# ConvNeXt-V2 block: three of eleven blocks kept whole in DRAM, the others recomputed whole

## The chip, the cores and the metric

One core of one Trainium2 chip. The time is the device time of one launch in microseconds (us). The kernel before has a median of 1508.93 us over 7 runs (1504.76 to 1513.4).

## The reference

`x` is a picture of 512 x 512 pixels with 96 channels in bf16. The block is a depthwise 3 x 3 convolution, a layer norm over the channels, a matmul to 384 channels, a tanh gelu, a global response norm (GRN) and a matmul back to 96 channels, with a residual:

```python
out = sum over i, j of xp[:, i:i+H, j:j+W, :] * dw[i, j]      # depthwise 3x3
h = _gelu(einsum('bhwc,ce->bhwe', _layernorm(out), w1))
gx = jnp.sqrt((h * h).sum(axis=(1, 2), keepdims=True) + 1e-6) # over the whole picture
nx = gx / (gx.mean(axis=-1, keepdims=True) + 1e-6)
h = grn_gamma * (h * nx) + grn_beta + h
return x + jnp.einsum('bhwe,ec->bhwc', h, w2)
```

`gx` needs the gelu outputs of every pixel before the second matmul can start. So the picture is gone over twice.

## The kernel before

The picture is cut into 128 blocks of 4 rows (2,048 pixels). A block is four quarters ("quads") of 512 pixels; the 384 middle channels are three chunks of 128 (`NCH`).

**First pass.** It runs in slots, about one block per slot, each engine following an order written out by hand (`InOrder`, so line 32, where the helper records the call, stands for most instructions). For slot s: SP loads x rows of block s+4 (`load_x`); VectorE transposes the rows of block s+2 into channel-major form (`turn_x`, into `xT`); TensorE does the convolution of block s from three neighbouring `xT` (`conv_taps`, into `Y`); ScalarE evacuates it (`y_bf`). GpSimd squares it (`ysq`), TensorE sums (`SG`), and every four blocks the reciprocal standard deviation is worked out on GpSimd (`stage_rstd`, `stage_newton`), turned by VectorE, written to DRAM and read back spread over the partitions (`rbc`, `stage_rows`, `stage_bcast`). GpSimd multiplies (`yn`, `stage_norm`), SP writes `yn` to DRAM (`stage_write`) and reads it back in channel order (`ynT`, `stage_read`).

A few slots later the block has its MLP (`mlp_units`): nine units, each some matmuls with `w1p` into a PSUM tile `U` of one or two banks, and one gelu on ScalarE. Quads 0 and 1 come channel-major into `gsh`, and quad 2 channel-major and quad 3 pixel-major into `gm`. The sum of squares for `gx` is taken in two ways. Channel-major quads get `bn_stats` on VectorE (`squares`, `squares_rest`, three per quad: nine a slot). The pixel-major quad gets Gram products on TensorE (`gram_mms`: 12 matmuls of 128 x 128 whose diagonal is the sum), half of them in each of two places of the next slot. `cm_quads` says how many quads of a block are channel-major: 3, and 2 for the last two blocks.

Quad 0 of each block is stored to DRAM by SP in the next slot (`store`, 384 KB of `g_dram`). The last two blocks (`RES`) keep two quads in SBUF (`resg`).

**Between the passes** VectorE turns the sums into the GRN scale and scales `w2` into `W2s`, while TensorE and ScalarE already recompute quads of the two resident blocks (`ahead`).

**Second pass.** The blocks are gone through in `ORDER`, the two resident ones first. At iteration n:
- `stage_load` (line 234) for block n+5: `gl`, the stored quad, on SP, or on GpSimd's queue for every third block (line 242); `ynT`, the other three quads of the normalised input, on SP (line 245), 768 bytes per row and partition; `xr`, the rows of x, on GpSimd's queue (line 247). `gl` has six buffers, `xr` five, `ynT` six.
- `stage_xb` (line 275) for block n+2: GpSimd adds the bias to `xr` (`xb`, line 279, three buffers).
- `stage_mm2` (line 283) for block n: four subs, each 12 matmuls with `W2s` into a tile `O`, VectorE adds `xb` to give `o_sb`, and then `pace` (line 331) issues further recompute units: three matmuls of 512 columns into `U` and one gelu of 1,536 elements per partition into `gr`. A block has three such units, each one chunk of channels over three quads.
- `stage_out` (line 309) writes the finished block on SP.

These second-pass DMAs and `xb` aren't under the hand-written order; the scheduler places them on their queues.

Of the kernel before, what the change touches and what calls it, by code (L numbers as in the profile page):

```python
# [9 lines left out]
ACTF = mybir.ActivationFunctionType  # L10
# [8 lines left out]
RES = 2  # L19

# [33 lines left out]
def kernel(  # L54
# [29 lines left out]
    g_dram = dram.tile([NBLK, 128, NCH * QW], bf16, name="g_dram")  # L84
# [5 lines left out]

    def cm_quads(q):
        return 2 if is_res(q) else 3

    def kept_quads(q):
        return 2 if is_res(q) else 1
# [16 lines left out]
    def yn_rows(q):  # L112
        k = kept_quads(q) * 128
        return yn_dram[q:q + 2].rearrange("q c (r w) -> (q c) r w", r=GR)[0:128, :, k:]
# [30 lines left out]
    res_g = {q: prepool.tile([128, 2, NCH, QW], bf16, name=f"resg{q}") for q in range(NBLK - RES, NBLK)}  # L145
# [7 lines left out]
    ORDER = list(range(NBLK - RES, NBLK)) + list(range(NBLK - RES))  # L153

    class late:
        pass
# [3 lines left out]
    with ExitStack() as p1:  # L160
        pe, dve, act, pool, sp = (InOrder(tc, e) for e in (nc.tensor, nc.vector, nc.scalar, nc.gpsimd, nc.sync))
        gshpool = p1.enter_context(tc.tile_pool(name="gsh", bufs=3))
        gmpool = p1.enter_context(tc.tile_pool(name="gm", bufs=3))
# [70 lines left out]
        def stage_load(n, sq, pq):  # L234
            q = ORDER[n]
            v = (ORDER[0] + n) % NYT
            r0 = q * GR
            if is_res(q):
                kept, ynt = res_g[q], ynts[q]
            else:  # L240
                kept = late.gl.tile([128, 1, NCH, QW], bf16, name="gl")
                (pq if q % 3 == 0 else sq).dma_start(  # L242
                    out=kept[:].rearrange("p t j w -> p (t j w)"), in_=g_dram[q])
                ynt = yn_ring[v]
                sq.dma_start(out=ynt[:, :, kept_quads(q) * 128:], in_=yn_rows(q))
            xr = late.xr.tile([128, PXP, C], bf16, name="xr")
            pq.dma_start(out=xr[:], in_=x[0, r0:r0 + GR].rearrange("r w c -> (r w) c").rearrange(  # L247
                "(p g) c -> p g c", g=PXP))
            grp[q] = dict(kept=kept, ynt=ynt, xr=xr)

        def recompute_units(q):
            nk = kept_quads(q)
            ynt = grp[q]["ynt"]

            def fresh(j):
                if j == 0:
                    grp[q]["made"] = late.gr.tile([128, NCH, (NQ - 1) * QW], bf16, name="gr")
                def half(U, t0, t1):
                    for t in range(t0, t1):
                        pe.matmul(quad_out(U[:, t - t0, :]), lhsT=w1p[:, j * 128:(j + 1) * 128],  # L260
                                  rhs=quad(ynt[:], t), start=True, stop=True)
                    act.activation(out=grp[q]["made"][:, j, (t0 - nk) * QW:(t1 - nk) * QW],
                                   in_=U[:, :t1 - t0, :].rearrange("p k w -> p (k w)"), func=ACTF.Gelu_apprx_tanh)

                if not is_res(q):
                    half(late.psU2.tile([128, NQ - 1, QW], f32, name="U2"), nk, NQ)
                elif j % 2:
                    half(banks(1), nk, nk + 1)
                    half(banks(1), nk + 1, NQ)
                else:  # L270
                    half(banks(2), nk, NQ)

            return [lambda j=j: fresh(j) for j in range(NCH)]
# [9 lines left out]
        def stage_mm2(n, q):  # L283
            kept, made, xb = grp[q]["kept"], grp[q]["made"], grp[q]["xb"]
            nk = kept_quads(q)
            GQ = QW // 128
            o_sb = late.o.tile([128, PXP, C], bf16, name="o_sb")
            for sub in range(NSUB):
                O = late.psO.tile([128, GPS, C], f32, name="O")
                for gl_ in range(GPS):  # L290
                    gg = sub * GPS + gl_
                    for j in range(NCH):
                        t, c = gg // GQ, gg % GQ * 128
                        if t < nk:
                            lhsT = kept[:, t, j, c:c + 128]
                        else:
                            c += (t - nk) * QW
                            lhsT = made[:, j, c:c + 128]
                        pe.matmul(O[:, gl_, :], lhsT=lhsT, rhs=W2s[:, j, :],
                                   start=(j == 0), stop=(j == NCH - 1))  # L300
                dve.tensor_tensor(out=o_sb[:, sub * GPS:(sub + 1) * GPS, :], in0=O[:],
                                   in1=xb[:, sub * GPS:(sub + 1) * GPS, :], op=ALU.add)
                if n == NBLK - 1:
                    out_part(q, o_sb, sub)
                pace(n, sub)
            grp.pop(q)
            return o_sb
# [8 lines left out]
        UPB = NCH  # L316
        LEAD = RES * UPB + 2
        todo = [n for n in range(NBLK) for _ in range(UPB)]
        total = len(todo)
        made = [0]  # L320
        waiting = []

        def advance(target, upto):
            while made[0] < total and made[0] < target and todo[made[0]] < upto:
                n = todo[made[0]]
                if not waiting:
                    waiting.extend(recompute_units(ORDER[n]))
                waiting.pop(0)()
                made[0] += 1

        def pace(n, sub):
            due = sum(1 for v in todo if v <= n + 1) if sub == NSUB - 1 else 0
# [287 lines left out]
        gms = {}  # L620
# [4 lines left out]

        def mlp_units(b):
            gsh = res_g[b] if is_res(b) else gshpool.tile([128, 2, NCH, QW], bf16, name="gsh")
            gms[b] = gmpool.tile([128, TAIL], bf16, name="gm")
# [5 lines left out]
            def unit(bank, n):  # L634
                U = banks(n)
                if bank < 2 * NCH:
# [3 lines left out]
                    act.activation(out=gsh[:, t0:t0 + n, j, :], in_=U[:], func=ACTF.Gelu_apprx_tanh)  # L640
# [4 lines left out]
                while c < end:  # L645
                    if c < px0(b):
                        j, sz = c // QW, QW
                        cm_mm(Uf[:, c - c0:c - c0 + sz], j, 2)
# [8 lines left out]
                act.activation(out=gms[b][:, c0:end], in_=Uf, func=ACTF.Gelu_apprx_tanh)  # L657

            def entry(j, m, src):
# [3 lines left out]
                dve.bn_stats(out=bsts[k][:, j, e, :], in_=src)  # L663

            def squares(j):
                for m in range(2):
                    entry(j, m, gsh[:, m, j, :])

            def squares_rest():
                if px0(b):  # L670
                    for j in range(NCH):
                        entry(j, 2, gms[b][:, j * QW:(j + 1) * QW])

            def store():
                sp.dma_start(out=g_dram[b], in_=gsh[:, 0].rearrange("p j w -> p (j w)"))

            return unit, squares, squares_rest, store

        def gram_mms(b, part=None):
            n = (TAIL - px0(b)) // E  # L680
            for k in range(n) if part is None else range(n // 2) if part == 0 else range(n // 2, n):
                for j in range(NCH):
                    c = px0(b) + k * E + j * 128
                    v = gms[b][:, c:c + 128]
                    pe.matmul(gram[:, j, :], lhsT=v, rhs=v, start=False, stop=True, skip_group_check=True)
# [17 lines left out]
        for k, (b0, n) in enumerate(BATCHES):  # L703
# [16 lines left out]
            for b in range(b0, b0 + n):  # L720
# [7 lines left out]
                put(m, "combine", b)  # L728
                put(m + (b < NBLK - 1), "gram", b)
# [5 lines left out]
        store = None  # L735
        for s in range(last_slot + 1):
# [11 lines left out]
            if store:  # L748
                store()
                store = None  # L750
# [18 lines left out]
            if not mlp:  # L769
                if s + 2 < NBLK:  # L770
                    turn_x(s + 2)
# [19 lines left out]
                for b in get("gram"):  # L791
                    gram_mms(b)
            else:
                b = mlp[0]
                unit, squares, squares_rest, put_out = mlp_units(b)
                conv = lambda n, fence=True: taps[n](fence) if taps else None

                def gram_of_last(part):
                    for b2 in get("gram"):
                        if b2 != b:  # L800
                            gram_mms(b2, part)
# [7 lines left out]
                if s + 2 < NBLK:  # L809
                    turn_x(s + 2)  # L810
# [3 lines left out]
                gram_of_last(0)  # L814
# [8 lines left out]
                gram_of_last(1)  # L823
# [7 lines left out]
                squares_rest()  # L831
                for b2 in get("gram"):
                    if b2 == b:
                        gram_mms(b2)
                if not is_res(b):
                    store = put_out
# [8 lines left out]
            if s == last_slot - 3:  # L845
# [4 lines left out]
                late.gr = p2.enter_context(tc.tile_pool(name="gr", side="right", bufs=4))  # L850
                late.gl = p2.enter_context(tc.tile_pool(name="gld", side="right", bufs=6))
# [6 lines left out]
        if store:  # L858
            store()
# [28 lines left out]
        ahead = [f for n in range(RES) for f in recompute_units(ORDER[n])]  # L888
        for f in ahead[:-1]:
            f()  # L890
# [16 lines left out]
        ahead[-1]()  # L907
        made[0] = RES * UPB
# [53 lines left out]
```

## Time and profile before

| | |
|---|---|
| median of 7 runs | 1508.93 us |
| the profiled execution | 1507.57 us, its span 1505.8 us |
| PE busy | 1414.8 us (94%) |
| ACT busy | 1451.5 us (96%) |
| DVE busy | 1194.0 us (79%) |
| POOL busy | 1309.8 us (87%) |
| DMA moved | 427.10 MB, 284 GB/s on average |

PE is TensorE, ACT ScalarE, DVE VectorE, POOL GpSimd, SP the sync engine that issues DMAs. The busy tenths in 40 slices of the span show the two passes: DVE falls at the 25th slice, DMA rises to 9 there:

```profile
DVE  7759999999999999999999989755555555455555
ACT  7898999999999999999999999999999999899997
POOL 3469899999999999999999987299999999899998
...
DMA  6668787888887887888888677899999999999996
```

The first pass ends at about 965 us, the second runs from about 972 us. Busy counts an engine that runs an instruction, so several engines can be full at once. What sets the time is read from the waits, stage by stage.

### The profile page before, as it was taken

How to read it: one execution, taken by the hardware profiler on the slowest of the kernel's cores; microseconds unless marked ns; L12 is line 12 of the kernel's file. 1: busy time of each engine (PE TensorE's matmuls, PEld its weight loads, DVE VectorE, ACT ScalarE, POOL GpSimd, SP SyncE). 2: the span in 40 equal slices, each digit the busy share in tenths (PEclk: the TensorE clock that was granted, in tenths of full speed). 3: DMA queues.
4: the chain of work that ended last, by engine and by line, in shares of the span. 5: the costliest groups of instructions: out<-in, count | busy, mean ns of one | idle time of the engine just before them, and what ended most of it. 6: DMA issues, size and time to landing. Idle time of an engine off the chain costs nothing. (4 is left out here: it accounts for less than half of the span.)

```text
span 1505.8 us, 54858 instructions
## 1 busy us (share of the span) xinstructions
PE 1414.8 (94%) x23110; PEld 815.7 (54%) x23110; DVE 1194.0 (79%) x2149; ACT 1451.5 (96%) x1699; POOL 1309.8 (87%) x934
## 2 busy tenths in 40 slices
PE   8888999999999999999999987799999999999998
PEld 3434444444444444444444443477777776676766
DVE  7759999999999999999999989755555555455555
ACT  7898999999999999999999999999999999899997
POOL 3469899999999999999999987299999999899998
PEclk9999999999999999999999999999999999999999
DMA  6668787888887887888888677899999999999996
GB/s 177 177 189 258 238 254 240 255 255 242 251 250 245 251 254 237 256 262 247 251 265 248 206 206 249 260 342 391 377 385 390 375 378 378 364 367 383 378 378 237
DMA packets 235181, 427.10 MB, mean 284 GB/s; under 512 B 34006, under 2 KB 148278, under 8 KB 234934
## 3 DMA queue, kind: packets, MB, share of 16 engines
q1 hardware_dynamic: 219972, 356.59, 73.3%
q0 software_dynamic: 13600, 66.86, 11.7%
q8 instruction: 181, 2.97, 0.8%
q14 instruction: 66, 0.54, 0.1%
q10 hardware_dynamic: 1362, 0.15, 0.1%
HBM read 272.78 MB, written 150.72 MB: 281 GB/s over the span
## 5 line engine op out<-in xcount | busy, mean ns | idle before, releaser
L32 PE MATMUL U<-ynT,w1p 128*128 128x512 bf16 x2292 | 650.6, 381 | 38.7 <-ACT gsh L32 9.1
L32 ACT ACTIVATE gr<-U 128x1536 bf16<-128x1536 f32 (+1 forms) x386 | 519.1, 1449 | 12.5 <-PE U L32 10.8
L32 DVE BATCH_NORM_STATS2 bst<-gsh 128x6 f32<-128x512 bf16 x756 | 465.6, 673 | 17.6 <-ACT gsh L32 17.3
L32 DVE TENSOR_TENSOR o_sb<-O,xb 128x384 bf16<-128x384 f32 x512 | 278.0, 556 | 252.7 <-PE O L32 156.9
L32 POOL TENSOR_TENSOR yn<-y_bf,rbc 128x1536 bf16<-128x1536 bf16 x126 | 391.3, 3108 | 74.5 <-ACT rbc L32 21.8
L32 ACT ACTIVATE gm<-U 128x512 bf16<-128x512 f32 (+1 forms) x640 | 419.8, 801 | 5.9 <-PE U L32 5.7
L279 POOL TENSOR_TENSOR xb<-xr,B2c 128x1536 f32<-128x1536 bf16 x126 | 394.7, 3133 | 32.3 <-DVE B2c L32 26.5
L32 ACT ACTIVATE gsh<-U 128x1024 bf16<-128x1024 f32 x504 | 375.1, 871 | 7.5 <-PE U L32 5.6
L32 PE MATMUL Y<-xT,Wq 64*32 64x511 bf16 (+1 forms) x8694 | 321.7, 387 | 20.0 <-ACT y_bf L32 8.5
L32 POOL TENSOR_TENSOR ysq<-y_bf 128x1536 bf16<-128x1536 bf16 x114 | 313.6, 2752 | 11.4 <-ACT y_bf L32 11.4
L32 PEld LDWEIGHTS <-w1p 128*128 128x128 bf16 x2292 | 182.9, 98 | 242.7 <-issue 151.0
L32 PEld LDWEIGHTS <-gr 128*128 128x128 bf16 x4584 | 237.1, 98 | 106.1 <-issue 20.3
L32 PE MATMUL O<-W2s,gr 128*128 128x96 bf16 x4584 | 257.6, 206 | 11.4 <-DVE o_sb L32 10.8
L32 DVE BATCH_NORM_STATS2 bst<-gm 128x6 f32<-128x512 bf16 x378 | 232.9, 672 | 0.2 <-ACT gm L32 0.2
L32 PEld LDWEIGHTS <-Wq 64*32 64x32 bf16 x9216 | 112.9, 90 | 196.6 <-issue 148.5
L32 ACT ACTIVATE y_bf<-Y 128x1536 bf16<-128x1536 f32 x121 | 188.1, 1554 | 7.9 <-PE Y L32 4.0
L32 DVE STREAM_TRANSPOSE xT<-xin 128x576 f32<-128x576 f32 (+1 forms) x256 | 181.3, 749 | 0.0
L32 PEld LDWEIGHTS <-gm 128*128 128x128 bf16 x1560 | 99.7, 98 | 85.5 <-issue 53.5
L32 PE MATMUL SG<-gm 128*128 128x128 bf16 x1560 | 130.7, 221 | 1.8 <-DVE SG L32 1.2
L32 PE MATMUL U<-w1p,ynT 128*128 128x384 bf16 (+2 forms) x780 | 127.2, 272 | 1.4 <-ACT resg L32 0.2
L247 POOL DMA_DIRECT2D xr<-in_x_dram x123 | 68.1, 554 | 38.5 <-POOL xb L279 35.3
L32 PE MATMUL O<-W2s,gl 128*128 128x96 bf16 x1512 | 85.0, 206 | 0.0
(105 smaller groups left out, 673.4 us busy)
## 6 DMA issues: line engine op xcount, KB each, us to landing
ynT<-yn_dram SPq DMA_DIRECT2D x254, 384.0 KB
xin<-in_x_dram SPq DMA_DIRECT2D x126, 432.0 KB
yn_dram<-yn SPq DMA_DIRECT2D x512, 96.0 KB
xr<-in_x_dram POOLq DMA_DIRECT2D x128, 384.0 KB, 6.5
out_dram<-o_sb SPq DMA_DIRECT2D x127, 384.0 KB
g_dram<-gsh SPq DMA_DIRECT2D x126, 384.0 KB
gl<-g_dram SPq DMA_DIRECT2D x84, 384.0 KB
gl<-g_dram POOLq DMA_DIRECT2D x42, 384.0 KB, 7.2
```

The lines of the kernel that those rows point to most:

```text
L32: r = f(*a, **k)
L247: pq.dma_start(out=xr[:], in_=x[0, r0:r0 + GR].rearrange("r w c -> (r w) c").rearrange("(p g) c -> p g c", g=PXP))
L279: pq.tensor_tensor(out=xb[:], in0=grp[q]["xr"][:], in1=bias[:, None, :].to_broadcast([128, PXP, C]), op=ALU.add)
```

## The change

Which quads are stored changes from "quad 0 of each block" to "all four quads of three blocks of eleven". `WHOLE = (0, 4, 8)` names them by block number modulo 11 (35 of 126). The other blocks store nothing, and all four of their quads are recomputed in the second pass, the last two blocks included (`resg` is gone).

- Channel-major quads: a whole block has four (all its quads are then in the layout that the second pass wants), the block after it two, others three. The last three `bn_stats` of a whole block are put off to the next slot (`square_owed`). Gram products go through a list (`gram_next`), two entries of six matmuls a slot.
- `gsh` and `gm` become one tile `g` with four buffers. A whole block is stored as two halves of 768 KB, one in each of the next two slots (`store_next`).
- `turn_x` runs three slots ahead instead of two.
- Second pass: `gl` is a whole block (1,536 KB, two buffers, always on GpSimd's queue); `ynT` is loaded whole (4,096 contiguous bytes per partition) for the other blocks. A recompute unit is one quad with its three chunks: three matmuls and one gelu of 1,536 as before. `gr` has three buffers of a block; `pace` spreads the units evenly over all subs and keeps at least two quads ahead of the use.

```diff
+WHOLE = (0, 4, 8)
+GRB = 3
...
     def cm_quads(q):
-        return 2 if is_res(q) else 3
+        return NQ if is_whole(q) else 2 if is_res(q) or (q - 1) % 11 in WHOLE else 3
...
         def stage_load(n, sq, pq):
...
+            if is_whole(q):
+                grp[q]["g"] = late.gl.tile([128, NQ, NCH, QW], bf16, name="gl")
+                pq.dma_start(out=grp[q]["g"][:].rearrange("p t j w -> p (t j w)"), in_=g_dram[whole.index(q)])
             else:
-                kept = late.gl.tile([128, 1, NCH, QW], bf16, name="gl")
-                (pq if q % 3 == 0 else sq).dma_start(
-                    out=kept[:].rearrange("p t j w -> p (t j w)"), in_=g_dram[q])
-                ynt = yn_ring[v]
-                sq.dma_start(out=ynt[:, :, kept_quads(q) * 128:], in_=yn_rows(q))
+                ynt = yn_ring[(ORDER[0] + nth_made[q]) % NYT]
+                if not is_res(q):
+                    sq.dma_start(out=ynt[:], in_=yn_rows(q))
...
+        def recompute(q, t):
...
+            for j0, n in ((0, NCH),) if late.psU2 else ((0, 2), (2, 1)):
+                U = late.psU2.tile([128, NCH, QW], f32, name="U2") if late.psU2 else banks(n)
+                for j in range(j0, j0 + n):
+                    pe.matmul(quad_out(U[:, j - j0, :]), lhsT=w1p[:, j * 128:(j + 1) * 128],
+                              rhs=quad(ynt[:], t), start=True, stop=True)
+                act.activation(out=g[:, t, j0:j0 + n, :], in_=U[:, :n, :], func=ACTF.Gelu_apprx_tanh)
...
+        LEAD = 5
+        todo = [(n, t) for n in range(NBLK) if not is_whole(ORDER[n]) for t in range(NQ)]
...
+                if n >= upto or nth_made[ORDER[n]] >= used[0] + GRB:
+                    break
...
-            due = sum(1 for v in todo if v <= n + 1) if sub == NSUB - 1 else 0
+            soon = (n, sub + 2) if sub < NSUB - 1 else (n + 1, 1)
+            due = sum(1 for v in todo if v < soon or v[0] < n)
...
+        def store_next():
+            if stores:
+                b, h = stores.pop(0)
+                n = NCH * QW * 2
+                sp.dma_start(out=g_dram[whole.index(b)][:, h * n:h * n + n],
+                             in_=gs[b][:, 2 * h:2 * h + 2].rearrange("p t j w -> p (t j w)"))
...
-            if store:
-                store()
-                store = None
+            store_next()
...
-                if s + 2 < NBLK:
-                    turn_x(s + 2)
+                if s + 3 < NBLK:
+                    turn_x(s + 3)
...
-                squares_rest()
...
+                squares_rest(2)
+                square_owed()
+                if is_whole(b):
+                    owed.append(lambda f=squares_rest: f(3))
+                grams.extend((b, k) for k in range(0, (TAIL - px0(b)) // E, 2))
+                if is_whole(b):
+                    stores.extend(((b, 0), (b, 1)))
...
-                late.gr = p2.enter_context(tc.tile_pool(name="gr", side="right", bufs=4))
-                late.gl = p2.enter_context(tc.tile_pool(name="gld", side="right", bufs=6))
+                late.gr = p2.enter_context(tc.tile_pool(name="gr", side="right", bufs=GRB))
+                late.gl = p2.enter_context(tc.tile_pool(name="gld", side="right", bufs=2))
```

## The prediction

> **What bounds the kernel now.** First the busy time by stretch (engine: busy us and instructions of each stretch), one stretch of the first pass and one of the second:
>
> ```profile
> 500.00:600.00 100.00, 96.43 (x1749) 47.03 (x1741) 99.44 (x173) 99.77 (x142) 93.97 (x76) 1.00 0.80 247
> ...
> 1050.00:1100.00 50.00, 50.00 (x714) 36.88 (x711) 27.36 (x50) 50.00 (x39) 46.20 (x29) 1.00 1.03 375
> ```
>
> The columns are PE, PEld, DVE, ACT, POOL, clock, DMA share, GB/s. In the first pass ACT (99.77 of 100) and DVE (99.44) have no idle time; in the second DVE is half idle, and PE, ACT, POOL and DMA all look full. So each pass is read by its waits. First pass, waits of ACT from 300 to 900 us; then second pass, waits of DVE and of POOL from 1000 to 1450 us:
>
> ```profile
> ACT gm L32 <- PE U L32: 2.2, 2, 1.3
> ACT gsh L32 <- ACT gm L32: 1.1, 4, 0.5
> ...
> DVE o_sb L32 <- PE O L32: 130.7, 251, 1.7
> DVE o_sb L32 <- POOL xb L279: 84.1, 78, 3.5
> ...
> POOL xr L247 <- POOL xb L279: 31.5, 106, 0.3
> POOL xr L247 <- issue: 2.9, 1, 2.9
> ```
>
> ACT waits about 3 us in 600: the first pass is ACT's, 7.06 us a slot (600 us, 85 blocks). In the second pass DVE waits for POOL's xb, while POOL waits for nobody but itself: every xr issue stands 0.3 us behind the xb before it. POOL's timeline there:
>
> ```profile
> 1097.32 3.13 POOL L279 TENSOR_TENSOR xb<-xr,B2c 128x1536 f32<-128x1536 bf16 x1
> 1100.75 0.55 POOL L247 DMA_DIRECT2D xr<-in_x_dram  x1 [0.30 <-POOL xb L279]
> 1101.32 3.14 POOL L279 TENSOR_TENSOR xb<-xr,B2c 128x1536 f32<-128x1536 bf16 x1
> 1104.76 0.55 POOL L247 DMA_DIRECT2D xr<-in_x_dram  x1 [0.30 <-POOL xb L279]
> 1105.34 3.14 POOL L279 TENSOR_TENSOR xb<-xr,B2c 128x1536 f32<-128x1536 bf16 x1
> 1108.77 0.55 POOL L247 DMA_DIRECT2D xr<-in_x_dram  x1 [0.30 <-POOL xb L279]
> 1109.32 0.54 POOL L242 DMA_DIRECT2D gl<-g_dram  x1
> 1109.87 3.13 POOL L279 TENSOR_TENSOR xb<-xr,B2c 128x1536 f32<-128x1536 bf16 x1
> ```
>
> There is no hole: three blocks take 12.55 us (1097.32 to 1109.87), 4.18 a block, made of 4.005 for xb, wait and xr, and 0.54 for one gl in three blocks. PE alone would go at 4.03 (its block starts there are 1099.81, 1103.79, 1107.82, 1111.85), and ACT, at 27.00 us for 20 gelus of 1,536, at 3 x 1.345 = 4.03. So POOL sets the second pass, with PE and ACT 4% behind. DMA moves 379 GB/s from 1000 to 1450 us, close behind too.
>
> **What the Trainium skill says.** "DMA: Bandwidth & Descriptors", section on queues, rings and completion order: each DMA engine takes turns between the queues that have work, a packet at a time. The trace's records of single packets agree: at 1109 to 1114 us, packets of POOL's queue (6,144 bytes) and SP's (3,072 and 768) run side by side, POOL's at about 25 a us, 157 GB/s. Same page, on why small descriptors are slow: a fixed overhead per packet. The records agree: from 1000 to 1450 us a 768-byte packet took 36.4 ns (21.1 GB/s on its engine), a 3,072-byte one 129.8 ns (23.7), a 6,144-byte one 250.5 ns (24.5). Same page, anatomy of a SWDGE DMA: a POOL DMA costs some 2 us and its bytes over 436 GB/s, and descriptor generation is small. The page of this kernel has 6.5 us from issue to landing of an xr, where that gives 2.9: the engines are shared, so I use the trace.
>
> **The change, part by part**
>
> *First pass, ACT.* The same nine gelus and one evacuation per slot, same sizes: nothing. *DVE.* Per eleven blocks 3 x 4 + 3 x 2 + 5 x 3 = 33 quarters get bn_stats, as before; the last three of a whole block go to the next slot, whose own block has only two quarters, so each slot keeps nine. Over all blocks 383 quarters instead of 382: three more at 0.58 us (spacing in DVE's timeline), 1.7 us. *PE.* A px-major quarter costs six pieces of 1,536 columns in all, a channel-major one three of 512; the slot after a whole block gets one more px-major quarter, the whole one's slot one less. Gram products stay 12 a slot through the list. PE's slack (its waits sum to 8 us in 600) covers such 0.2 us shifts; if not, ACT waits that much in three slots of eleven.
>
> *Transposes one slot earlier.* xin(s+4) is issued at slot s and turned at s+1 instead of s+2. In the trace an xin issue at 605.63 is turned at about 624.3; now at 617.3, 11.7 us later instead of 18.7. Landing is not shown; eight packets of 3,456 bytes per engine at 181 ns are 1.5 us, plus what is queued ahead. Between 0 and some us in a slot; I take 0.
>
> *Stores.* 126 x 384 KB become 70 halves of 768 KB, in the two slots after a whole block, each at the place where the old store stood on SP. Such a slot moves about 384 KB more than now (some 280 GB/s instead of 247), the others 384 KB less. Behind a store stand the next xin, the ynT read and, every fourth slot, rbc, for which POOL's yn already waits now and then (11.2 us from 200 to 940 us). POOL is nearly full too: 4 x 5.84 + 4.5 = 27.9 us of work per 28.2 us of four slots. It can gain where slots without a store let such a wait go, at most those 11 us, and lose in store slots; I take 1 us lost in all, and keep 0.2 us for each of 70 slots, 14 us, for the range.
>
> *Second pass, ACT and PE.* 372 quads of 3 matmuls and one gelu instead of 382; in the loop 32 per 11 blocks instead of 33, at most three in any block, since the pace is even over blocks. ACT: 32/11 x 1.345 = 3.91 us a block. PE: 4 x 0.51 for the O products and 32/11 x 0.65 for U, 3.93. A quad is always issued two quads ahead of its use, and psU2 has two buffers, so no new wait for gelu.
>
> *POOL.* This is where the time is. The instruction order of the changed kernel, which can be read without running it, has 33 gl (all on POOL, 1,536 KB each) between the third xb and the last but four, where before had 40; and after each gl but one two xb follow each other and then two xr. The second xr's 0.30 us wait is gone in 32 such pairs, and xb after xb starts 3.09 us after the first (five take 15.45 at the end of the trace) instead of 3.13. Check on before: 121 x 4.005 + 40 x 0.54 = 506.2, and the waits of 3.5 for o_sb and 2.9 for issue make 512.6; the trace has 972.14 to 1484.25, 512.1. After: 506.2 - 7 x 0.54 - 32 x 0.34 = 491.5, that is 14.7 us less, 4.06 a block. A gl of 128 rows of 12,288 bytes instead of 3,072 is not in the trace: at least 0.54 (cost by rows, as xr and gl show), at most 2.14 (by bytes), which adds 53 us. I take 0.54: the skill calls descriptor generation small. Two waits are new in that order, each with the next xb behind it: gl waits for PE's last use of the gl two before, four or more blocks back, which xb's own wait for o_sb covers; and one xr in each turn waits for the landing of the gl eight DMAs earlier, about six blocks back. Both 0.
>
> *DMA.* 1,597 KB a block (8 x 524 for ynT, 3 x 1,573 for gl, 11 x 786 for xr and out, over 11) instead of 1,573. In packet times: before 512 x 36.4 ns for ynT (18.6 us), 16.4 gl, 16.0 xr, 16.6 out, 67.7 us a block over 16 engines: 4.23, which is 1.01 of 4.18 (packets overlap). After, with 170 ns for a 4,096-byte packet (estimated between the rates of 3,072 and 6,144 bytes): 8 x 21.8 + 3 x 64.1 + 11 x 32.6 = 725 us per 11 blocks, 4.12 a block, 1.01 of 4.06, as the 768-byte packets are gone. So DMA stays as full as it is, at the faster pace: 393 GB/s, where 1000 to 1050 us had 391.
>
> *Ends.* The tail after the last xb (o_sb, out) is POOL's too and stays; the turn between the passes keeps its twelve early chunks: 0.
>
> Sum: 1.7 + 1 - 14.7 = -12.0 us. PE and ACT, now 3 to 4% behind POOL, and DMA, as full as before, may take a part back where they meet; that goes into the range. Span 1505.8 -> 1493.8; that execution took 1507.57, the median is 1508.93, so 1497.
>
> **Rivals**
>
> *DMA takes POOL's place.* For: 393 GB/s is above the mean of 379. Against: no engine waited for a load in steady state, and larger packets. At 391 GB/s a block takes 4.08 (1499); at 385, 4.15, and 11 of the 14.7 us are gone (1508).
>
> *Slower: a whole gl stands in front of xr on POOL's queue, and POOL waits at xb.* When the two xr are issued, gl has run for 6.6 us; at 25 packets a us 91 of its 256 packets are left, and the second xr's end comes after 91 + 128 packets, 8.8 us, and 2 more to land, with 12.3 us (three xb) until its like is needed. It decides once POOL's queue gets less than some 115 GB/s. One us late per gl is 33 us: 1530.
>
> *The first pass pays for the bursts.* ACT has no slack there, so 0.2 us in each of 70 store slots takes all back, and more: 1511.
>
> **How the numbers follow.** A measurement of this kernel tells 0.3% (4.5 us) from no change. Forecast 0.62, 1489 to 1504. DMA 0.13, half of it faster and half the same. Bursts 0.11, half same and half slower. Slower by gl on POOL, or its issue by bytes, 0.14. Faster 0.68, same 0.12, slower 0.20. The range reaches down for waits of the first pass that go, and up to bursts at their bound with a little of the gl case: 1487 to 1517.
>
> **What would show it.** Right: xb starts 4.06 us apart on average, pairs of xb 3.1 apart, gl about 0.54, first-pass slots still 7.06, ACT without waits there. Wrong: gl of 1 us or more on POOL; POOL xb waiting for DMA xr; ACT or POOL yn waiting for DMA in the first pass; PE U waiting for ynT.

## The result, and the profile after

The changed kernel has a median of 1503.84 us over 14 runs (1496.47 to 1507.7); the kernel before, over 35 runs, 1509.07 us. The ratio is 0.9951, with a 95% interval of 0.9936 to 0.9966: 5 to 10 us faster than before at that interval's ends, 7 in its middle. The forecast was 1497 us.

Three moments of the trace cut an execution into its parts: the start of the last `y_bf` on ACT ends the first pass, the first `o_sb` on DVE starts the second, and what lies between is called the turn here. (The turn so includes the last slots of the first pass, which still make `yn` and run the MLP of the last blocks.) In us, for the profiled executions:

| | first pass | turn | second pass | span |
|---|---|---|---|---|
| before | 877.6 | 97.0 | 531.2 | 1505.8 |
| after | 885.8 | 107.0 | 509.7 | 1502.4 |
| difference | +8.2 | +10.0 | -21.5 | -3.4 |
| forecast | +2.7 | 0 | -14.7 | -12.0 |

So a larger gain than forecast was made in the second pass, and most of it was given back ahead of it.

First the stretches that were shown of before, as before (PE, PEld, DVE, ACT, POOL, then clock, DMA share, GB/s):

```profile
500.00:600.00 100.00, 96.47 (x1762) 47.91 (x1748) 98.92 (x172) 100.00 (x143) 95.10 (x75) 1.00 0.84 259
1050.00:1100.00 50.00, 50.00 (x718) 36.83 (x716) 27.42 (x51) 49.94 (x38) 48.23 (x28) 1.00 1.02 407
```

What moved most is DMA, 407 GB/s instead of 375 in the second pass; POOL, at the faster pace, is busy for 48.23 of 50 us instead of 46.20. Once more it is the waits that tell.

**Second pass.** Waits of DVE, POOL and ACT of the changed kernel from 1000 to 1450 us (engine, line, what it waited for: us in all, times, longest):

```profile
DVE o_sb L34 <- PE O L34: 197.7, 324, 1.0
DVE o_sb L34 <- POOL xb L271: 3.3, 5, 0.7
...
POOL xr L252 <- POOL xb L271: 15.1, 51, 0.3
POOL xb L271 <- DVE o_sb L34: 4.0, 2, 3.8
...
ACT gr L34 <- ACT gr L34: 0.4, 1, 0.4
```

DVE's wait for `xb` fell from 84.1 to 3.3 us: POOL is no longer what comes last. From the first `o_sb` of block 20 to that of block 110, in the order of the second pass, it is 355.5 us instead of 377.0, 3.950 a block instead of 4.189; the figures "a block" below are taken in the same way. The whole gain of 21.5 us lies there. ACT waits for nobody, and the chain that ended last now goes through its gelus (part 4 of the page, its lines):

```profile
ACT gr L34 28%; PE O L34 2%; PE U L34 2%; DVE o_sb L34 0%; ACTq L34 0%; DVEq L34 0%
```

POOL's timeline there (start, us, instruction, how many, the idle time before it):

```profile
1108.93 0.53 POOL L245 DMA_DIRECT2D gl<-g_dram  x1
1109.48 6.21 POOL L271 TENSOR_TENSOR xb<-xr,B2c 128x1536 f32<-128x1536 bf16 x2
1115.63 1.10 POOL L252 DMA_DIRECT2D xr<-in_x_dram  x2
1116.75 3.14 POOL L271 TENSOR_TENSOR xb<-xr,B2c 128x1536 f32<-128x1536 bf16 x1
1120.18 0.55 POOL L252 DMA_DIRECT2D xr<-in_x_dram  x1 [0.30 <-POOL xb L271]
```

The `gl` of 1,536 KB costs 0.53 us to issue, like one of 384 KB. After it two `xb` and two `xr` stand together, and neither `xr` waits 0.30 us. The pair takes 7.27 us (1109.48 to 1116.75), where two single turns of 4.01 take 8.02.

**First pass.** Waits of PE, then of POOL, from 300 to 900 us, first before, then after:

```profile
PE SG L32 <- POOL ysq L32: 2.2, 2, 1.6
...
POOL yn L32 <- DMA g_dram<-gsh: 10.5, 9, 3.1
POOL yn L32 <- DMA rbc<-r_dram: 4.3, 3, 2.0
POOL yn L32 <- ACT gsh L32: 3.3, 3, 1.8
POOL yn L32 <- ACT gm L32: 2.5, 2, 1.5
```

```profile
PE SG L34 <- POOL ysq L34: 10.1, 8, 2.9
...
POOL yn L34 <- DMA rbc<-r_dram: 16.3, 12, 3.4
POOL yn L34 <- ACT g L34: 5.7, 3, 2.2
```

POOL waits for `rbc` at the first `yn` of a batch of four blocks. The waits that stand under other names, the store's or ACT's, come at the same `yn` in both kernels, so they are counted with it: 20.6 us before, 24.7 after. That is not much more. What is new is that PE now waits for POOL's squares, 10.1 us instead of 2.2. One such place in the timeline of PE:

```profile
748.56 0.45 PE L34 MATMUL SG<-rowsel,y_bf 128*128 128x4 bf16 x12
750.81 0.46 PE L34 MATMUL SG<-rowsel,ysq 128*128 128x4 bf16 x12 [1.81 <-POOL ysq L34]
751.13 0.38 PE L34 MATMUL U<-w1p,ynT 128*128 128x128 bf16 x2
751.44 1.05 PE L34 MATMUL Y<-xT,Wq 64*32 64x512 bf16 x24
752.59 1.46 PE L34 MATMUL U<-ynT,w1p 128*128 128x512 bf16 x3
753.98 1.48 PE L34 MATMUL Y<-xT,Wq 64*32 64x512 bf16 x24
755.39 0.82 PE L34 MATMUL U<-ynT,w1p 128*128 128x512 bf16 x3
```

After the 1.81 us, PE is slow as well: three matmuls of 512 take 1.46 us instead of 0.82, a convolution group 1.48 instead of 0.87. The busy time by stretch shows why; the last three numbers are the granted clock (the share of full speed that TensorE was given), the DMA share and GB/s:

```profile
748.00:752.00 4.00, 2.19 (x57) 1.38 (x54) 4.00 (x8) 3.50 (x5) 4.00 (x3) 1.00 0.89 280
752.00:756.00 4.00, 3.90 (x46) 0.91 (x31) 2.93 (x6) 1.83 (x4) 4.00 (x2) 0.57 0.86 265
```

The granted clock was 0.57 in the stretch after the stall, and ACT was busy for 1.83 of 4 us. The stall is paid twice. This is not one unlucky execution: the clock, averaged over an execution, was 0.984 to 0.991 in all of the changed kernel, and 0.989 to 0.997 in those of the kernel before that were taken with the experiments.

**The turn.** PE's timeline, then SP's waits from 940 to 975 us:

```profile
960.36 1.93 PE L34 MATMUL U<-ynT,w1p 128*128 128x512 bf16 x6
969.24 1.89 PE L34 MATMUL U<-ynT,w1p 128*128 128x512 bf16 x4 [6.95 <-DMA ynT<-yn_dram]
```

```profile
SPq L34 <- DMA yn_dram<-yn: 18.2, 5, 14.8
```

PE waits 6.95 us for the `ynT` of one of the last slots, because SP, which issues that read, waits 14.8 us for the write of `yn` ahead of it (the longest such wait was 6.0 us in the kernel before). The clock was low here too, 0.88 on average from 886 to 993 us; in the turn of the kernel before, 878 to 975 us, it was 0.96. What the DMA engines did meanwhile (queues from 945 to 965 us: packets, MB, share of the 16 engines):

```profile
q0 software_dynamic: 796, 5.69, 76.4%
q1 hardware_dynamic: 714, 1.59, 23.4%
...
gl<-g_dram POOLq DMA_DIRECT2D x1, 1536.0 KB, 11.0
```

POOL had issued seven `xr` and the first two whole `gl` on its queue (q0) by 957 us, in packets of 6,144 and 12,288 bytes (the `gl` in the view is the second one; the first was issued at 944.11). The writes of `yn` on SP's queue (q1) are packets of 1,024 bytes. The Trainium skill ("DMA: Bandwidth & Descriptors", section on queues, rings and completion order) says that an engine takes turns between its queues a packet at a time. By packet it means a group of some 9 to 17 descriptors, and the trace counts single runs of bytes, so the two can't be matched one to one; but turns between packets so unequal would give SP's queue the small part that it has here.

### The profile page after: what moved, and what is told of

Read it like the earlier page. It is cut to its first block, busy times and chain, and to the rows that moved or that the text cites. A ratio compares the mean times of both kernels' runs of the same rounds, so it can differ in the third digit from the quotient of the medians.

```text
span 1502.4 us, 54165 instructions
## 1 busy us (share of the span) xinstructions
PE 1408.7 (94%) x23065; PEld 813.0 (54%) x23065; DVE 1198.6 (80%) x2152; ACT 1440.2 (96%) x1689; POOL 1302.7 (87%) x927
## 5 line engine op out<-in xcount | busy, mean ns | idle before, releaser
L34 ACT ACTIVATE g<-U 128x512 bf16<-128x512 f32 (+1 forms) x1152 | 759.6, 834 | 27.5 <-PE U L34 15.3
L34 DVE BATCH_NORM_STATS2 bst<-g 128x6 f32<-128x512 bf16 x1149 | 694.9, 673 | 33.2 <-ACT g L34 32.8
L34 PE MATMUL U<-ynT,w1p 128*128 128x512 bf16 x2265 | 642.1, 384 | 40.4 <-ACT g L34 12.0
L34 ACT ACTIVATE gr<-U 128x1536 bf16<-128x1536 f32 (+1 forms) x376 | 506.2, 1444 | 5.3 <-PE U L34 2.5
L34 PEld LDWEIGHTS <-gr 128*128 128x128 bf16 x4464 | 221.0, 98 | 65.2 <-issue 1.3
L34 PE MATMUL O<-W2s,gr 128*128 128x96 bf16 x4464 | 236.4, 206 | 0.2 <-DVE o_sb L34 0.2
L34 PEld LDWEIGHTS <-g 128*128 128x128 bf16 x1548 | 97.4, 98 | 81.4 <-issue 51.9
L34 PE MATMUL SG<-g 128*128 128x128 bf16 x1548 | 127.0, 220 | 1.9 <-DVE SG L34 1.5
L34 PEld LDWEIGHTS <-gl 128*128 128x128 bf16 x1680 | 82.8, 98 | 23.2 <-issue 0.5
L34 PEld LDWEIGHTS <-ynT 128*128 128x128 bf16 x774 | 61.4, 99 | 28.4 <-issue 9.7
```

Of the source, the lines that this page charges most:

```text
L34: r = f(*a, **k)
```

## The experiments

The theory after these readings: the second pass gained because POOL was relieved; the turn lost because the first whole `gl` move on POOL's queue beside the last writes of `yn`; the first pass lost because `rbc` comes late. Rivals were that DMA bounds the second pass, that the transposes one slot earlier cost the time, that the size of the stores does, and that a dip of the clock alone does.

**All `gl` on SP's queue.**

```diff
-                pq.dma_start(out=grp[q]["g"][:]..., in_=g_dram[whole.index(q)])
+                sq.dma_start(out=grp[q]["g"][:]..., in_=g_dram[whole.index(q)])
```

> The changed kernel with every gl on SP's queue instead of POOL's. Theory A (the turn: the first two gl, 3 MB in 12,288-byte packets on POOL's queue, take the DMA engines from the 1,024-byte yn writes in the last slots of the first pass, so SP sits 15 us on them and PE waits 7 us for ynT): the stretch from the last y_bf to the first o_sb falls from 107 us to 97 to 100, time about 8 us under the changed kernel, ratio to before about 0.990. Theory B (nothing is lost at the turn but by a dip of the clock in that one execution): the ratio stays at 0.995. For the second pass: if ACT sets it now (3.95 us a block, its chain of gelus), it stays at 3.95 although POOL is 0.15 us a block freer; if POOL still sets it, it falls to about 3.9.

Measured: 1495.4 us, ratio 0.9912 (0.9884 to 0.9939). The turn is back at 97.0 us. But the second pass has 511.9 us, 3.99 a block against 3.95, which neither forecast had: with no `gl` between them the `xb` stand alone again, and each `xr` waits its 0.30 us. DVE's wait for `xb` comes back with it (waits of DVE and POOL, 1000 to 1450 us):

```profile
DVE o_sb L34 <- POOL xb L271: 25.6, 27, 3.3
...
POOL xr L252 <- POOL xb L271: 32.7, 110, 0.3
```

One stretch of this run tells what sets the 3.95 of the other versions. From block 20 to block 65 it went at 3.94 a block too, as the changed kernel did, while DVE hardly waited for `xb` (2.7 us from 1055 to 1230 us), as some were made ahead; the 4.03 of POOL's single turns came after that. So where POOL holds nothing up, PE and ACT allow 3.94, with pairs or without.

**Only the `gl` issued before and around the turn on SP's queue.**

```diff
-                pq.dma_start(out=grp[q]["g"][:]..., in_=g_dram[whole.index(q)])
+                (sq if n <= 6 else pq).dma_start(out=grp[q]["g"][:]..., in_=g_dram[whole.index(q)])
```

> The changed kernel with only the gl of the first two whole blocks on SP's queue, the other 33 on POOL's. Theory A: the same gain as with all of them moved, within 2 us, since only these two lie in the turn. If the gain of moving all is larger by 4 us or more, POOL's queue costs something in the second pass too. Theory B: 0.995 as the changed kernel.

Measured: 1496.14 us, 0.9911 (0.9879 to 0.9944); turn 94.7, second pass 508.7, 3.950 a block. Only two `gl` move, those of the first two whole blocks. Both gains are had at once, though the median doesn't tell this version from the last. SP's longest wait for `yn` in the turn is 5.8 us instead of 14.8, and the clock there is 0.98. Moving these two `gl` is enough to take the turn's loss away; it is not the only way, as the fourth edit shows.

**The kernel before with every `gl` on SP's queue.** This takes all 42 issues of `gl` off POOL (40 of them in the stretch that the forecast summed) and puts these transfers among those of SP's queue.

```diff
-                (pq if q % 3 == 0 else sq).dma_start(
+                sq.dma_start(
```

> The kernel before with every gl on SP's queue (42 of 126 were on POOL's). If POOL's queue (xb, wait, xr, gl) set the second pass before, it goes from 4.18 to 4.03 us a block, where ACT and PE stand: 121 x 0.15 = 18 us less, ratio 0.988. If DMA set it, 4.18 stays and the ratio is 1.00.

Measured: 1492.09 us, 0.9885 (0.9857 to 0.9912); second pass 516.7 us instead of 531.2, 4.035 a block instead of 4.189. POOL's queue did set the second pass, and without those issues it runs at the 4.03 that the gelus (and PE) allow. A one-word edit gives 14.5 of the 21.5 us.

**`rbc` ahead of the read of `ynT`.** In each slot SP issues the broadcast of the statistics first.

```diff
+            for k in get("bcast"):
+                stage_bcast(k)
             for b in get("read"):
                 stage_read(b)
             for b in get("write"):
                 stage_write(b)
-            for k in get("bcast"):
-                stage_bcast(k)
```

> The changed kernel with the four rbc loads put on SP ahead of the slot's ynT read and yn write. Theory C (the first pass lost about 8 us because POOL's yn waits for rbc, so ysq is late and PE's SG sums wait, 10.1 us from 300 to 900 us): POOL's waits for rbc and PE's waits for ysq go, 6 to 8 us less than the changed kernel, ratio about 0.990. Rival (the loss is of a dip of the clock or of PE in slots with two px-major quarters): waits of POOL go, time as the changed kernel.

Measured: 1483.52 us, 0.9834 (0.9806 to 0.9861); first pass 872.1 us instead of 885.8. Waits of PE, then of POOL, from 300 to 870 us:

```profile
PE Y L34 <- ACT y_bf L34: 3.7, 24, 0.2
PE SG L34 <- DVE SG L34: 0.8, 3, 0.5
...
POOL yn L34 <- DMA rbc<-r_dram: 6.3, 6, 2.3
```

PE's waits for the squares are gone, and ACT waits for nothing in this stretch. The gain is 20 us, where 6 to 8 were expected. The first pass gained 9.6 us over 96 evacuations in its steady part (below) and 4.4 before that, and the turn gained as well, 98.7 us instead of 107.0, with the `gl` where they were. So either edit takes most of the turn's loss away, and the two overlap: by these profiles, moving the two `gl` is worth 12.3 us without `rbc` first and 5.7 with it (98.7 to the 93.0 below). What shrank in the turn is the slow clock, 0.97 instead of 0.88, and PE's longest wait for `ynT`, 4.3 us; SP's longest wait for `yn` stayed, at 17.5. Why the waits at `yn` reach PE in the changed kernel and hardly did before, where they were nearly as long, no run shows.

**The transposes of x two slots ahead again** (two places and the start-up):

```diff
-                if s + 3 < NBLK:
-                    turn_x(s + 3)
+                if s + 2 < NBLK:
+                    turn_x(s + 2)
```

> The changed kernel with the transposes of x back at two slots ahead. Theory C (the first pass loses through late rbc rows on SP's queue): the transposes have nothing to do with it, first pass and time as the changed kernel (last y_bf near 886 us, ratio 0.995). Rival D (the loads of x, now needed a slot earlier, come late for the transposes and cost the first pass its 8 us): last y_bf falls to about 878 us, ratio 0.990.

Measured: 1494.77 us, 0.9923 (0.9897 to 0.9949). The profiled execution has the first pass of the changed kernel, 885.8 us, and took 1502.98; five others took about 1494 to 1496. The interval overlaps the changed kernel's. This run alone decides nothing; the last one below does, for the kernel with `rbc` first.

**`rbc` first and the first `gl` on SP's queue**, the second and fourth edit together:

> The changed kernel with both cures: rbc loads first in the slot, and the gl of the first two whole blocks on SP. If they act on different stretches, the turn falls from 98.7 us to about 95 and the rest stays as with the rbc cure alone: 3 to 4 us less than that, ratio about 0.981. If the earlier rbc has cured the turn as well (SP comes to its ynT read sooner), nothing more is won: 0.983.

Measured: 1477.15 us, 0.9801 (0.9777 to 0.9825), the fastest of all. First pass 872.7, turn 93.0, second pass 508.4. The clock was 0.996 to 1.000 in its executions. The times that showed the stall and the slow clock above, in this kernel, which is some 10 us further on by then (PE alone: busy, clock, DMA share, GB/s):

```profile
748.00:752.00 4.00, 3.88 (x70) 1.00 0.55 175
752.00:756.00 4.00, 3.73 (x77) 1.00 0.74 196
```

**The kernel before with both edits** (`rbc` first, every `gl` on SP):

> The kernel before with every gl on SP and with the rbc loads first in the slot. If the storing of whole blocks is worth only what it takes off ACT and PE in the second pass (4.035 to 3.95 us a block), this one stands 8 to 10 us behind the changed kernel with both cures: ratio about 0.987, first pass about 4 us shorter than before. If the first pass of before gains nothing from rbc (its POOL waits cost no time), it stays at 0.9885.

Measured: 1484.56 us, 0.9848 (0.9825 to 0.9872). Against the run before this one that leaves 0.0047, about 7 us, for storing whole blocks as such, with intervals that just touch. The trace has it in the second pass: 515.5 against 508.4 us, 4.034 against 3.950 a block; 32 units in place of 33 would by themselves give 3.91. The two differ in one thing more: this one has every `gl` on SP's queue, the other only the first two.

**Stores in three parts of 512 KB instead of two of 768**, with a fifth buffer of `g` to hold the block a slot longer:

```diff
-        gpool = p1.enter_context(tc.tile_pool(name="g", bufs=4))
+        gpool = p1.enter_context(tc.tile_pool(name="g", bufs=5))
...
-                n = NCH * QW * 2
+                n = NCH * QW * NQ // 3
...
-                    stores.extend(((b, 0), (b, 1)))
+                    stores.extend(((b, 0), (b, 1), (b, 2)))
```

> The changed kernel with each whole block stored in three parts of 512 KB in three slots instead of two halves of 768 KB, and five buffers of g instead of four so that the third store has time. If the size of the stores in a slot makes rbc late (the bursts), the first pass gains about half of its loss, last y_bf at 880 to 882 us, ratio 0.992 or less. If it is not the bursts, it stays at 886 us and 0.995.

Measured: 1499.71 us, 0.9941 (0.9919 to 0.9963), not to be told from the changed kernel. The profiled first pass is shorter, 881.4 us; but kernels with the changed kernel's own first pass have 881.8 and 885.0 (the two with moved `gl`), so one profile can't carry that. From the 33rd to the 129th evacuation of `y_bf` (of 135: seven blocks have theirs in two parts) it has 668.1 us, against 677.4 in the changed kernel, and 4.0 us more before that (170.2 against 166.2), where its clock was 0.95 instead of 0.99: a hint that smaller stores help in the steady part. Whether they do stays open.

**`rbc` first, in the kernel before, alone:**

> The kernel before with the broadcast of the statistics (rbc) issued ahead of the read of ynT in each slot, its gl still partly on POOL's queue. Theory (late rbc hurts only in the change's first pass, the kernel before loses little to it): first pass within 3 us of 877.6 (875 to 878), second pass 4.19 us a block, total 1503 to 1508. Rival (the wait for rbc cost the kernel before as much as it cost the changed one): first pass some 872, total near 1500 to 1503.

Measured: 1498.52 us, 0.9915 (0.9897 to 0.9933). The total is the rival's: the kernel before lost time to a late `rbc` as well. It did so in other places, though. From the 33rd to the 129th `y_bf` it takes 668.6 us, and the kernel before 669.1: nothing gained there. The gain lies in the first 33 (159.6 us instead of 166.2) and in the turn (92.9 instead of 97.0), and in both the clock was 1.00, where the kernel before had 0.98 and 0.96. POOL at the start, before and then in this run:

```profile
102.67 3.10 POOL L32 TENSOR_TENSOR yn<-y_bf,rbc 128x1536 bf16<-128x1536 bf16 x1 [9.05 <-DMA rbc<-r_dram]
```

```profile
97.53 3.11 POOL L32 TENSOR_TENSOR yn<-y_bf,rbc 128x1536 bf16<-128x1536 bf16 x1 [4.19 <-DMA rbc<-r_dram]
```

Over these 96 evacuations the changed kernel takes 677.4 us, and the runs with the same first pass and a moved `gl` 671.0 and 674.6; with `rbc` first it takes 667.8. In the changed kernel's record the clock stands at one half for 6.8 us of these 677.4, and in those with a moved `gl` for 3.4 and 6.8; in the kernel before and with `rbc` first it never does. At half speed 6.8 us lose at most 3.4 us of work. So, by this estimate, at least 4.9 of the 8.3 us over the kernel before were not lost to the clock, and a dip alone doesn't explain the loss.

**The fastest version with the transposes two slots ahead:**

> The changed kernel with rbc first and the first loads of gl on SP (1477.15 us), and in addition the transposes of x back to two slots ahead. Theory (turning x three slots ahead costs nothing once rbc is not late): 1475 to 1479, first pass 872 to 874. Rival (the transposes hold the first pass up on their own, as the runs of the other trial without a profile hinted): 1470 to 1473, first pass below 870.

Measured: 1481.18 us, 0.9803 (0.9781 to 0.9826), first pass 873.4 us. Against the kernel before, run beside it, it is where the version with three slots was, at 0.9801. So with `rbc` first the transposes cost nothing.

## Why the prediction was right and where it failed

The forecast of a small gain held, by the reason it gave, and the gain came out at some 7 us of 12 because three of its terms were mis-sized, in both directions. That the total came near is in part luck: the second pass gained 6.8 us more than forecast, and the first pass and the turn lost 15.5 us more. The measured 1503.84 lies at the upper edge of the 1489 to 1504 that the forecast gave its own case.

- *POOL sets the second pass*: right. The kernel before without `gl` on POOL shows it, 4.189 to 4.035 us a block.
- *32 pairs that lose one wait of 0.30 and start 0.04 earlier, 0.34 each*: too small. Both waits of a pair go, and a pair takes 0.75 us less in the timeline. The forecast's POOL, 4.06 a block, would then have been 4.06 - 3 x 0.41 / 11 = 3.95. PE and ACT are level with that, as the stretch of 3.94 without pairs shows, which is why all versions with pairs stop at 3.95 and the gain was 21.5 instead of 14.7 us. Which of the two holds the other is not settled: the chain that ended last goes through ACT's gelus in the changed kernel (28% of the span) and through PE alone in the fastest one (34%), at the same 3.950. The forecast's 3.91 for ACT and 3.93 for PE were that close. The sum also counted the gain over all 121 blocks; blocks 2 to 10 take 32.2 us in both kernels, and the gain came from the 90 blocks after the 20th.
- *gl's issue at 0.54 us whatever its size*: right, 0.53. The bound of 2.14 is not seen.
- *DMA as full as before, at a faster pace*: right, and the rival that DMA takes POOL's place is refuted for this pace: 407 GB/s from 1050 to 1100 us, where the forecast needed 393.
- *xr late behind a whole gl*: did not come. `xr` landed after 6.7 us in the median, and POOL's `xb` waits for no DMA in the steady part. (The forecast counted 256 packets for a `gl`; the trace has 128 of 12,288 bytes. And its bound for POOL's queue, 115 GB/s, is low by its own figures: the 91 and 128 packets of 6,144 bytes that it leaves for 12.3 less 2 us need 131 GB/s.)
- *Ends: 0*: wrong, +10.0 us. It counted the twelve early chunks, and not that the first two `gl` and seven `xr` run on POOL's queue while the last `yn` are still being written. Moving these two `gl` alone brought 107.0 to 94.7; `rbc` first alone brought it to 98.7, so the place of the `gl` cost this much only together with the late `rbc`. The rule that would explain it, turns by the packet, stood in the forecast, but was asked only about `gl` against `xr`, and not about the small packets on SP's queue.
- *Stores: 1 us*: wrong, +8.2 in the profile (2 to 8 us over the 96 evacuations in the three runs with this first pass). The waits were found, at `yn` for `rbc`, but only in part: 11.2 us from 200 to 940 us, where those under other names at the same `yn` add 18.3. POOL's load, 27.9 of 28.2 us in four slots, is too tight a sum, as POOL made up most of these waits in the kernel before. What was not drawn from them is that a wait which POOL doesn't make up leaves PE standing for `ysq`, and that the slow clock then adds to it. With `rbc` first the term is gone. In kind this is the rival of the bursts, at about half its 14 us; that the larger stores make `rbc` late is hinted at by the stores in three parts and not shown.
- *ACT's first pass is at its floor*: only in the steady part, 669.1 against 667.8 us. In the first 33 evacuations 6.6 us were to be had.
- *bn_stats put off to the next slot*: no wait of ACT for them above 1.6 us is in the trace (2.5 us in all); that part was not tried alone.

## What to carry to other kernels

Where engines are level, price a moved transfer by what it meets on the DMA engines at the ends of a stage, not only by its issue and its mean rate: here SP waited 14.8 us for small writes beside large packets on POOL's queue, and a chain of write, read and broadcast is made of such small ones. An engine with little to spare may pass a wait on to the next one; look for the wait's cause on the queue in front of it, where the order of a few issues was worth more here (`rbc` first took the changed kernel's ratio from 0.9951 to 0.9834) than the change itself. And before moving work off a full engine, try the edit that only moves its issues.

## What was not expected of the hardware

- After a wait of PE of 1.81 us, which ended at 750.81, the granted clock was 0.57 from 752 to 756 us, and it was 0.50 from 970 to 976 us after the 6.95 us wait. The Trainium skill ("TensorE: Matmul & The Clock Gate", part 1, the clock gate) has half rate after an idle window of about 3.4 us; the second agrees, the first came after a shorter wait, with only small matmuls just before and just after it.
- A `gl` of four times the bytes took the same time to issue on POOL, 0.53 us, and one core moved 407 GB/s from 1050 to 1100 us.
- Two `xr` in a row behind two `xb` wait for neither; one behind one waits 0.30 us. Taking the DMA between them away made the second pass slower, 3.95 to 3.99 us a block.
